# A Fourier mixer and a low-rank mixer on one core: U's rows turned by an f32 product, signed table copies on ACT, folds and column loads held in written order, three o buffers

## The chip, the cores and the metric

The kernel runs on one core of one Trainium2 chip. A core has five engines, each with its own instruction stream in order: PE (matrix products into PSUM, with the weight loads PEld beside them), DVE (elementwise work), ACT (functions and copies), POOL (elementwise work, and the issue of some transfers) and SP (the issue of transfers). Sixteen DMA engines carry the transfers of all queues. The metric is the device time in microseconds (us) of one execution; less is better.

## What is computed

For each of 8 batches of `x` (3136 rows n, 256 columns d, f32), a Fourier transform along both axes, of which the real part is kept, then a low-rank mixing over the rows, and a two-layer network over the columns:

```python
X = np.fft.fft(x, axis=1); X = np.fft.fft(X, axis=2); x = X.real
xt = x.transpose(0, 2, 1)
h = xt @ U @ V                      # U: 3136 x 32, V: 32 x 3136
u = x + h.transpose(0, 2, 1)
ch = np.maximum(u @ w_ch1, 0.0) @ w_ch2     # 256 x 1024, 1024 x 256
out = u + ch
```

## The kernel before, in words

**Setup (lines 90 to 676, an order written by hand).** The transform along the rows is a product with tables of sines (`tabs[0]`, in the profile `tabs`) and cosines (`tabs[1]`, in the profile `tabc`), eight row tiles i of 98 or 99 partitions each. DVE makes phases (`phase`, L166 and L168: `pho` for even i with 786 values, `phe` for odd i with 394), ACT their sine (L173). Other parts of the tables are copies of cells with the sign kept or changed: `mirror_even` on ACT (L255), `cosine_odd` and `cosine_turned` on POOL, where a kept sign is a copy (L260) and a changed one a multiplication by -1 (L262). For tiles 7 and 3 cosines come from ACT (L179, L180).

Symmetry halves the work: rows n and S-n are added and subtracted ("folded") before the product, and so are columns d and 256-d. So each batch of `x` is loaded twice, forward with its partitions in turned order (`xf`, by a gather with an index list that POOL issues, `load_f`), and from the other end (`xr`, plain transfers, `load_r`). The same is done for U: `UF` is gathered by POOL (two gathers, L111), `UR` is loaded by SP. `fold_u` (L191, L194) makes `GU` from both, and `transform_u` appends the transform of U to the tables in four steps: `contract` (PE, L219), `keep` (ACT, L225), `turn` (PE, L232), `evict` (ACT, L237, L238). `halve` (L243) scales tile 7 of a table.

**Per batch (`transform(b)`).** Eight fold steps: for each half a of the rows, `alone` (two columns, POOL, L284) and `along_d` (DVE, L278 and L280) on `xf` and on `xr`, then `mirror` (DVE, L287) twice; then `half` (DVE, L291) twice into `G[b % 2]`. Eight `seq` steps multiply G with the tables (PE, L328), with a copy on ACT (L332) and sums on DVE (L335 to L346). Eight `chan` steps (PE, L452 and L454; ACT, L456) and `lowrank` finish the batch. `load_x(b + 1)` stands after the folds of b.

**Chunks.** The 8 x 3136 rows of the result are 49 chunks of 512. `front(c)` makes `u` of a chunk (PE, L496; DVE, L504) and its transpose `ut` by a transfer that SP issues (L507). `first_product` (PE, L516; ACT, L518) is called eight times a chunk, `second_product` (PE, L532) four times; after every second one DVE adds `ut` to the product in `p2` and writes `o` (L538 to L541), and after the fourth SP issues the transfer of `o` to the output (L546). Of `u`, `p2` and `o` there are two buffers each, of `p1`, `ut` and the PSUM tiles called dft three.

**What sets the order.** The last loop writes chunk c's first products and chunk c-1's second products into eight slots per chunk, adds the steps that the table `due` has for each slot, and calls `front(c + 1)` at slot 3. Batch b's steps are spread evenly over slots from 8*((b-1)*3136//512)+4 to 8*(b*3136//512-1)+3, so the folds of batch 1 begin at slot 4, of batch 2 at 59 (six column steps stand ahead of them), of batch 3 at 100. Up to the end of chunk 0 the program's order is kept as written. From c == 1 on (`order.close()`) a planner may change it: for each engine it takes, when by its own estimate the engine is free, the instruction written first among those whose inputs are ready.

**Column loads.** The column 128 of batches 2 to 7 is treated apart; SP loads it with 28 transfers of single 4-byte elements (`column_loads`, L383 and L391) into `cf` and `cr`, eight in the setup and one in each slot from slot 8 on. `fl` and `flip` are 0/1 matrices with which a product turns the order of partitions (L407, L410).

Of the kernel before, what the change touches and what calls it, by code (L numbers as in the profile page):

```python
# [13 lines left out]
AL = mybir.AluOpType  # L14
# [13 lines left out]
def kernel(  # L28
# [18 lines left out]
    cpool = ctx.enter_context(tc.tile_pool(name="cpool", bufs=1))  # L47
    psum = ctx.enter_context(tc.tile_pool(name="psum", bufs=1, space=bass.MemoryType.PSUM))
# [34 lines left out]
    def load_x(b):  # L83
        for a in range(2):
# [12 lines left out]
    krow = cpool.tile([P, 2, NQ], FP32, name="krow")  # L97
# [5 lines left out]
    nc.gpsimd.iota(xidx[:], pattern=[[S // 8, B], [S // 16, 2]], base=97, channel_multiplier=-1)  # L103
    load_0f(moe_U, UF, 0, R, nc.scalar)
# [13 lines left out]
    fsel = cpool.tile([P, 2, 2, R], FP32, name="fsel")  # L118
    sel = cpool.tile([P, 2, 2 * R], BF16, name="sel")
    nc.gpsimd.iota(fsel[:], pattern=[[R, 2], [2 * R, 2], [1, R]], base=0, channel_multiplier=-1,  # L120
                   allow_small_or_imprecise_dtypes=True)
    lrow = cpool.tile([P, 2, P], FP32, name="lrow")
    pcol = cpool.tile([P, 1], FP32, name="pcol")
# [35 lines left out]
    wp = ctx.enter_context(tc.tile_pool(name="wp", bufs=2))  # L159
    setup = ExitStack()  # L160
    gen = setup.enter_context(tc.tile_pool(name="gen", bufs=2))
# [25 lines left out]
    GU = [cpool.tile([KP, 2, NI, R], BF16, name=f"gu{par}", tag=f"gu{par}") for par in range(2)]  # L187
# [62 lines left out]

    def mirror_even(t, i):

        odd_m = (i + 1) // 2 % 2 == 1
        sgn = 1.0 if odd_m == (t == 0) else -1.0
        nc.scalar.activation(cells(t, i, 0, 1, NH - 1, 1), cells(t, i, NQ - 1, -1, NH - 1, 0),  # L255
                             AF.Copy, scale=sgn)

    def pool_copy(dst, src, sgn):
        if sgn > 0:
            nc.gpsimd.tensor_copy(dst, src)  # L260
        else:
            nc.gpsimd.tensor_single_scalar(dst, src, -1.0, op=AL.mult)  # L262
# [12 lines left out]
    def along_d(a, src, dst, part):  # L275
        lo, hi = src[:, a, :, 1:128], src[:, a, :, 255:128:-1]
        if part == 0:
            nc.vector.tensor_tensor(dst[:, a, :, 1:128], lo, hi, op=AL.subtract)  # L278
        else:
            nc.vector.tensor_tensor(dst[:, a, :, 129:256], lo, hi, op=AL.add)  # L280

    def alone(a, src, dst):

        nc.gpsimd.tensor_copy(dst[:, a, :, 128:257:128], src[:, a, :, 0:129:128])  # L284

    def mirror(a, cols, op):
        nc.vector.tensor_tensor(EOS[:, a, :, cols], EOF_[:, a, :, cols],  # L287
                                EOR_[:, a, ::-1][:, :, cols], op=op)

    def half(b, par, cols):  # L290
        nc.vector.tensor_tensor(G[b % 2][par][:, :, cols], EOS[:, 0, :, cols],  # L291
                                EOS[:, 1, :, cols], op=AL.add if par == 0 else AL.subtract)
# [67 lines left out]
    fl = cpool.tile([P, 2, P], FP32, name="fl")  # L360

    def column_setup():

        nc.gpsimd.iota(fl[:, 0], pattern=[[1, P]], base=-(PQ - 1), channel_multiplier=1,
                       allow_small_or_imprecise_dtypes=True)
        nc.gpsimd.iota(fl[:, 1], pattern=[[1, P]], base=0, channel_multiplier=-1,
                       allow_small_or_imprecise_dtypes=True)

# [4 lines left out]
    def column_flips():  # L373
        nc.vector.tensor_single_scalar(flip[:], fl[:], 0.0, op=AL.is_equal)
        nc.vector.tensor_copy(flip[:KP, 0, PQ:KP], flip[:KP, 1, PQ:KP])
        nc.vector.tensor_copy(unit[:], flip[:, 1, :NB])

    def column_loads():

        for t, dst, n in ((0, cf, NI - 1), (1, cr, 0)):  # L380
            for a in range(2):
                def edge(dst=dst, n=n, a=a):
                    nc.sync.dma_start(out=dst[PQ:KP, a, n, :],  # L383
                                      in_=bass.AP(x.tensor, x.offset + (B0 * S + a * HALF) * D + P,
                                                  [[D, 1], [S * D, NB]]))
                yield edge
            for b in range(NB):
                for a in range(2):
                    def load(t=t, dst=dst, b=b, a=a):
                        n0 = 1 + a * HALF if t == 0 else S - 784 - a * HALF  # L390
                        nc.sync.dma_start(  # L391
                            out=dst[:PQ, a, :, b],
                            in_=bass.AP(x.tensor, x.offset + ((B0 + b) * S + n0) * D + P,
                                        [[8 * D, PQ], [D, NI]]))
# [339 lines left out]
```

## Time and profile before

| | us |
|---|---|
| three runs | 495.13, 502.37, 510.74 |
| median | 502.37 |
| the profiled execution | 499.26 |
| its span in the profile | 497.3 |
| PE busy in the span | 460.0 (93%) |
| DVE busy | 321.2 (65%) |
| ACT busy | 279.6 (56%) |
| POOL busy | 82.3 (17%) |
| first `pt` product (L328) starts | 28.53 |
| first first product (L516) starts | 47.87 |

The span is the time from the first to the last instruction of the profiled execution; some 2 us lie around it. Busy time of PE has matrix products that overlap, so it is not PE at its peak. In a timeline, a row gives the start and the duration in us, the engine, the line of the kernel, the operation, the tile written and the tile read, and in brackets the time that the engine had been idle and what it waited for. In a table of windows, each row gives the stretch, its length, the busy time of each engine in it, the granted clock of PE (1.00 is full speed), the share of the DMA engines that is busy, and GB/s.

### The profile page before, as it was taken

To read this page: it belongs to the slowest core of one execution; us is meant where nothing else is said; L and a number is where in the kernel's file an instruction comes from. 1 tells how busy PE (TensorE), PEld (TensorE's weight loads), DVE (VectorE), ACT (ScalarE), POOL (GpSimd) and SP (SyncE) were. 2 spreads that over 40 slices of the span, in tenths; PEclk is the share of its full clock that TensorE was granted. 3 is DMA by queue.
4 is the path that set the end of the run, shared out by engine and by line. 5 is a ranking of instruction groups with operands and counts; after the bars stand their busy time and mean duration, and the time that the engine had idled before them with its cause. 6 is when DMAs were issued, how large, how long until landed. Compare 5 with 4: busy or idle time off the path is not lost.

```text
span 497.3 us, 7932 instructions
## 1 busy us (share of the span) xinstructions
PE 460.0 (93%) x3001; PEld 288.4 (58%) x3001; DVE 321.2 (65%) x712; ACT 279.6 (56%) x531; POOL 82.3 (17%) x126
## 2 busy tenths in 40 slices
PE   0378789989999999999999999999999999999997
PEld 0133446645656666666666666666666666666665
DVE  9997978799899988793474436444534444344343
ACT  4724533745646655665557554766466555655662
POOL 8973612121222331110000000000000000000000
PEclk9999979999999999999999999999999999999999
DMA  8689797989996989425323332333322532333433
GB/s 203 155 118 220 125 183 122 223 220 220 143 307 142 253 229 275 133 66 128 81 69 107 81 110 65 84 107 86 106 65 73 119 86 65 105 86 106 129 86 127
DMA packets 103492, 67.24 MB, mean 135 GB/s; under 512 B 73572, under 2 KB 99898, under 8 KB 100302
## 3 DMA queue, kind: packets, MB, share of 16 engines
q1 hardware_dynamic: 97512, 40.50, 37.2%
q0 software_dynamic: 5920, 26.24, 20.2%
q8 instruction: 23, 0.38, 0.3%
q14 instruction: 15, 0.12, 0.1%
q10 hardware_dynamic: 22, 0.00, 0.0%
HBM read 29.33 MB, written 25.69 MB: 111 GB/s over the span
## 4 chain that ended last, share of the span: by engine, by line
PE 66%; DVE 19%; DMA 10%; issue 3%; POOL 1%; SPq 0%; DVEq 0%; ACT 0%; ACTq 0%
PE p L532 27%; PE p L516 26%; PE pt L328 7%; DMA out_dram<-o 6%; DMA xf<-in_x_dram 3%; PE ph L496 3%; DVE u L504 2%; DVE eor L278 2%; DVE eof L278 2%; DVE eor L280 2%; PE pst L452 1%; PE pst L454 1%; DVE eos L287 1%; DVE eof L280 1%; DVE phe L166 1%
## 5 line engine op out<-in xcount | busy, mean ns | idle before, releaser
L518 ACT ACTIVATE h<-p 128x512 bf16<-128x512 f32 x392 | 218.9, 597 | 141.7 <-PE p L516 141.4
L516 PE MATMUL p<-u,w 128*128 128x512 bf16 x784 | 211.3, 380 | 6.2 <-DVE u L504 6.2
L532 PE MATMUL p<-w,h 128*128 128x256 bf16 x1568 | 204.6, 273 | 0.0
L532 PEld LDWEIGHTS <-h 128*128 128x128 bf16 x1568 | 153.5, 98 | 60.6 <-issue 0.9
L516 PEld LDWEIGHTS <-w 128*128 128x128 bf16 x784 | 75.5, 98 | 70.1 <-DVE u L504 6.3
L538 DVE TENSOR_TENSOR o<-p,ut 128x4 f32<-128x4 f32 (+1 forms) x100 | 16.3, 163 | 135.1 <-PE p L532 129.7
L328 PEld LDWEIGHTS <-g 98*128 98x128 bf16 (+1 forms) x288 | 28.8, 101 | 29.2 <-DVE g L291 4.5
L541 DVE TENSOR_TENSOR o<-p,ut 128x254 f32<-128x254 f32 (+1 forms) x100 | 40.7, 407 | 0.0
L540 DVE TENSOR_TENSOR o<-p,ut 128x254 f32<-128x254 f32 (+1 forms) x100 | 40.7, 407 | 0.0
L328 PE MATMUL pt<-tabc,g 98*128 98x425 bf16 (+1 forms) x160 | 37.4, 360 | 1.9 <-DVE g L291 1.1
L504 DVE TENSOR_TENSOR u<-ph,S 128x512 bf16<-128x512 f32 (+15 forms) x64 | 35.1, 557 | 1.9 <-DMA xf<-in_x_dram 1.7
L504 DVE TENSOR_TENSOR u<-ph,T 128x512 bf16<-128x512 f32 (+15 forms) x64 | 34.9, 556 | 0.0
L332 ACT COPY ev<-pt 128x425 f32<-128x425 f32 x32 | 16.5, 515 | 31.4 <-PE pt L328 18.1
L328 PE MATMUL pt<-tabs,g 98*128 98x425 bf16 (+1 forms) x128 | 30.3, 362 | 3.0 <-DVE g L291 2.5
L496 PE MATMUL ph<-va,ta 128*128 128x512 bf16 (+18 forms) x128 | 29.6, 329 | 0.5 <-DVE B L346 0.5
L335 DVE TENSOR_TENSOR tab<-pt,ev 128x32 bf16<-128x32 f32 x32 | 6.1, 190 | 28.3 <-PE pt L328 28.2
L52 POOL DMA_INDIRECT xf<-in_x_dram,xidx x16 | 18.1, 1128 | 36.8 <-DVE eof L280 26.5
L287 DVE TENSOR_TENSOR eos<-eof,eor 99x1024 bf16<-99x1024 bf16 (+2 forms) x34 | 22.3, 688 | 0.2
L452 PE MATMUL pst<-A,mc 128*128 128x392 bf16 (+1 forms) x64 | 21.1, 330 | 1.3 <-DVE u L504 0.9
L454 PE MATMUL pst<-B,msn 128*128 128x392 bf16 (+1 forms) x64 | 21.1, 330 | 0.0
L456 ACT CAST S<-pst 128x392 bf16<-128x392 f32 (+1 forms) x32 | 15.6, 489 | 8.8 <-PE pst L454 8.6
L278 DVE TENSOR_TENSOR eof<-xf 99x1016 bf16<-99x1016 f32 x16 | 19.3, 1207 | 1.7 <-DMA xf<-in_x_dram 1.7
(126 smaller groups left out, 305.8 us busy)
## 6 DMA issues: line engine op xcount, KB each, us to landing
out_dram<-o SPq DMA_DIRECT2D x48, 512.0 KB
xr<-in_x_dram POOLq DMA_DIRECT2D x14, 784.0 KB, 8.8
xr<-in_x_dram SPq DMA_DIRECT2D x2, 784.0 KB
ut<-u SPq DMA_TRANSPOSE x49
w<-in_moe_w_ch_dram POOLq DMA_DIRECT2D x1, 512.0 KB, 6.4
out_dram<-o SPq DMA_DIRECT2D x4, 128.0 KB
va<-in_moe_V_dram POOLq DMA_DIRECT2D x2, 196.0 KB, 7.2
xf<-in_x_dram,xidx POOLq DMA_INDIRECT x16, 9.8
```

Of the source, the lines that this page charges most:

```text
L278: nc.vector.tensor_tensor(dst[:, a, :, 1:128], lo, hi, op=AL.subtract)
L287: nc.vector.tensor_tensor(EOS[:, a, :, cols], EOF_[:, a, :, cols], EOR_[:, a, ::-1][:, :, cols], op=op)
L328: nc.tensor.matmul(pt[:], g[:kp(i), i, col:col + P], tabs[t][:kp(i), i, par, :], start=(n == 0), stop=(n == len(mm) - 1))
L452: nc.tensor.matmul(pt[:, :hi - lo], MC[:, h * P:(h + 1) * P], d["A"][:, lo:hi], start=True, stop=False)
L454: nc.tensor.matmul(pt[:, :hi - lo], MSN[:, h * P:(h + 1) * P], d["B"][:, lo:hi], start=False, stop=True)
L496: nc.tensor.matmul(ph[:, col:col + hi - lo], TA[b % 2][:, s * P:(s + 1) * P], VA[b % 2][:, lo:hi], start=True, stop=True)
L504: nc.vector.tensor_tensor(u[:, s, col:col + hi - lo], ph[:, col:col + hi - lo], src, op=AL.add)
L516: nc.tensor.matmul(p1[:], W1[:, s, j * P:(j + 1) * P], k["u"][:, s, :], start=(s == 0), stop=(s == 1))
L518: LAST[0] = nc.scalar.activation(k["h"][:, j, :], p1[:], AF.Relu)
L532: nc.tensor.matmul(p2[:, t % w, :], h[:, j, rs], W2[:, j, :], start=(j == 0), stop=(j == JT - 1))
L540: nc.vector.tensor_tensor(o[:, ts, 1:P], p2[:, :w, 1:P], ut[:, ts, 1:P], op=AL.add)
L541: nc.vector.tensor_tensor(o[:, ts, P + 1:D], p2[:, :w, P + 1:D], ut[:, tT, P - 1:0:-1], op=AL.add)
```

## The change

U's forward rows come in their own order by a plain transfer of SP (no gather), and PE turns them with `fl`, a 0/1 matrix in f32, in one f32 product of 99 x 99 by 99 x 512 into PSUM (`turn_u`); `fold_u` reads that. `fl` is therefore made early (POOL writes the index values, DVE compares), and `flip` becomes a copy of it. Table copies with a changed sign run on ACT, those with a kept sign on POOL (`turned_copy`; one kept sign, of tile 3 of the cosines, on ACT), and are written in another order among the sines. Tiles that only the setup uses move from the lasting pool to the one that is closed after the setup, and `o` gets three buffers. From chunk 1 on, `pin` holds every instruction of the folds and every column load behind the instruction written just ahead of it on its engine (issue order only; it adds no wait for a result). Column loads stand in every second slot instead of every one. In `column_loads` both transfers are held.

```diff
+    wp = ctx.enter_context(tc.tile_pool(name="wp", bufs=2))
+    setup = ExitStack()
+    gen = setup.enter_context(tc.tile_pool(name="gen", bufs=2))
...
-    UF = cpool.tile([KP, 2, NI, R], FP32, name="uf")
-    UR = cpool.tile([KP, 2, NI, R], FP32, name="ur")
...
+    UF = gen.tile([KP, 2, NI, R], FP32, tag="uf", name="uf", bufs=1)
+    UR = gen.tile([KP, 2, NI, R], FP32, tag="ur", name="ur", bufs=1)
...
-    nc.sync.dma_start(out=UR[:PQ].rearrange("p a i d -> p a (i d)"),
-                      in_=bass.AP(moe_U.tensor, moe_U.offset + (S - 784) * R,
-                                  [[8 * R, PQ], [-HALF * R, 2], [1, 8 * R]]))
-    for a in range(2):
-        gather(UF[:PQ, a].rearrange("p i d -> p (i d)"), moe_U, S // 8 - 1,
-               xidx[:PQ, 0, a:a + 1], 8 * R, R)
+    for t, n0, step in ((UF, 1, HALF), (UR, S - 784, -HALF)):
+        nc.sync.dma_start(out=t[:PQ].rearrange("p a i d -> p a (i d)"),
+                          in_=bass.AP(moe_U.tensor, moe_U.offset + n0 * R,
+                                      [[8 * R, PQ], [step * R, 2], [1, 8 * R]]))
...
+    nc.gpsimd.iota(fl[:, 0], pattern=[[1, P]], base=-(PQ - 1), channel_multiplier=1,
+                   allow_small_or_imprecise_dtypes=True)
+    nc.gpsimd.iota(fl[:, 1], pattern=[[1, P]], base=0, channel_multiplier=-1,
+                   allow_small_or_imprecise_dtypes=True)
...
+    TURNED = []
+
+    def turn_u():
+        nc.vector.tensor_single_scalar(fl[:], fl[:], 0.0, op=AL.is_equal)
+        nc.vector.tensor_copy(fl[:KP, 0, PQ:KP], fl[:KP, 1, PQ:KP])
+        pf = psum.tile([KP, 2, NI, R], FP32, tag="dft", name="pf", bufs=3)
+        nc.tensor.matmul(pf.rearrange("p a i r -> p (a i r)"), fl[:KP, 0, :KP],
+                         UF.rearrange("p a i r -> p (a i r)"), start=True, stop=True)
+        TURNED.append(pf)
 
     def fold_u(typ):
         h = (uo, ue)[typ]
-        nc.vector.tensor_tensor(h[:], UF[:], UR[:, :, ::-1, :],
+        nc.vector.tensor_tensor(h[:], TURNED[0][:], UR[:, :, ::-1, :],
                                 op=AL.subtract if typ == 0 else AL.add)
...
+    def turned_copy(dst, src, sgn):
+
         if sgn > 0:
             nc.gpsimd.tensor_copy(dst, src)
         else:
-            nc.gpsimd.tensor_single_scalar(dst, src, -1.0, op=AL.mult)
+            nc.scalar.activation(dst, src, AF.Copy, scale=-1.0)
+
...
+    def mirror_even(t, i):
+
+        odd_m = (i + 1) // 2 % 2 == 1
+        turned_copy(cells(t, i, 0, 1, NH - 1, 1), cells(t, i, NQ - 1, -1, NH - 1, 0),
+                    1 if odd_m == (t == 0) else -1)
 
     def cosine_odd(i):
 
-        pool_copy(cells(1, i, 1, 1, NQ - 1, 0), cells(0, i, NQ - 2, -1, NQ - 1, 1),
-                  1 if i % 4 == 0 else -1)
-
-    def cosine_turned(i):
-
-        sgn = 1 if i == 1 else -1
-        pool_copy(cells(1, i, NH - 1, 1, NH, 1), cells(0, i, NQ - 1, -1, NH, 0), sgn)
-        pool_copy(cells(1, i, 0, 1, NH - 1, 1), cells(0, i, NH - 1, 1, NH - 1, 1), -sgn)
+        turned_copy(cells(1, i, 1, 1, NQ - 1, 0), cells(0, i, NQ - 2, -1, NQ - 1, 1),
+                    1 if i % 4 == 0 else -1)
+
+    def cosine_low(i):
+
+        turned_copy(cells(1, i, NH - 1, 1, NH, 1), cells(0, i, NQ - 1, -1, NH, 0),
+                    1 if i == 1 else -1)
+
+    def cosine_high(i):
+
+        turned_copy(cells(1, i, 0, 1, NH - 1, 1), cells(0, i, NH - 1, 1, NH - 1, 1),
+                    -1 if i == 1 else 1)
+
+    PIN = []
+
+    def pin(ins):
+
+        if PIN:
+            tc.keep_in_program_order(ins)
 
...
+            pin(nc.vector.tensor_tensor(dst[:, a, :, 1:128], lo, hi, op=AL.subtract))
...
+        pin(nc.gpsimd.tensor_copy(dst[:, a, :, 128:257:128], src[:, a, :, 0:129:128]))
...
+        pin(nc.vector.tensor_tensor(EOS[:, a, :, cols], EOF_[:, a, :, cols],
+                                    EOR_[:, a, ::-1][:, :, cols], op=op))
...
+        pin(nc.vector.tensor_tensor(G[b % 2][par][:, :, cols], EOS[:, 0, :, cols],
+                                    EOS[:, 1, :, cols], op=AL.add if par == 0 else AL.subtract))
...
-        nc.vector.tensor_single_scalar(flip[:], fl[:], 0.0, op=AL.is_equal)
-        nc.vector.tensor_copy(flip[:KP, 0, PQ:KP], flip[:KP, 1, PQ:KP])
-        nc.vector.tensor_copy(unit[:], flip[:, 1, :NB])
+        nc.vector.tensor_copy(flip[:], fl[:])
+        nc.vector.tensor_copy(unit[:], fl[:, 1, :NB])
...
+                        pin(nc.sync.dma_start(
                             out=dst[:PQ, a, :, b],
                             in_=bass.AP(x.tensor, x.offset + ((B0 + b) * S + n0) * D + P,
-                                        [[8 * D, PQ], [D, NI]]))
...
-            k["o"] = cp.tile([P, CH // P, D], FP32, tag="o", name="o", bufs=2)
+            k["o"] = cp.tile([P, CH // P, D], FP32, tag="o", name="o", bufs=3)
...
-    for m, i in enumerate(range(0, NI, 2)):
+    def odd_row(m, i):
         phase(pho[:, m], krow[:KP], ncol[:KP, i:i + 1], 15)
         sine(tabs[0][:, i, :, :NQ], pho[:, m], 15, 1)
-        cosine_odd(i)
+
+    for m, i in ((0, 0), (1, 2)):
+        odd_row(m, i)
+    cosine_odd(2)
+    for m, i in ((2, 4), (3, 6)):
+        odd_row(m, i)
+    cosine_odd(6)
     for m, i in enumerate((7, 5, 3, 1)):
         phase(phe[:, m], krow[:KP, :, NH - 1:], ncol[:KP, i:i + 1], 15)
         sine(tabs[0][:, i, :, NH - 1:NQ], phe[:, m], 15, 1)
-        mirror_even(0, i)
+        if m == 0:
+            mirror_even(0, 7)
+            turn_u()
+        if i == 5:
+            cosine_high(5)
+            mirror_even(0, 5)
+        if i == 3:
+            mirror_even(0, 3)
+    cosine_low(1)
+    mirror_even(0, 1)
+    for i in (0, 4):
+        cosine_odd(i)
     fold_u(0)
     halve(0)
...
+    us, uc = transform_u(0), transform_u(1)
+    us[0]()
+    cosine(tabs[1][:, 7, :, NH - 1:NQ], phe[:, 0], 15)
+    mirror_even(1, 7)
+    cosine(tabs[1][:, 3, :, NH - 1:NQ], phe[:, 2], 15)
+    nc.scalar.copy(cells(1, 3, 0, 1, NH - 1, 1), cells(1, 3, NQ - 1, -1, NH - 1, 0))
+    us[1]()
+    us[2]()
+    cosine_low(5)
+    cosine_high(1)
+    us[3]()
     for a in range(2):
...
-    for i in (5, 1):
-        cosine_turned(i)
     nc.gpsimd.dma_start(out=W1[:, 0, :], in_=moe_w_ch1[0:P, :])
     w1t = gen.tile([P, H], FP32, name="w1t", tag="w1t", bufs=1)
     gather(w1t[:], moe_w_ch1, D, pint[:], H, 0)
+    for a in range(2):
+        alone(a, xf, EOF_)
     nc.gpsimd.memset(VA[0][:].bitcast(I32), 0)
     nc.gpsimd.dma_start(out=VA[0][:R, :], in_=moe_V)
+    nc.gpsimd.dma_start(out=W2[:], in_=moe_w_ch2.rearrange("(j p) d -> p j d", p=P))
     column_zeros()
-    for a in range(2):
-        alone(a, xf, EOF_)
-    nc.gpsimd.dma_start(out=W2[:], in_=moe_w_ch2.rearrange("(j p) d -> p j d", p=P))
-    column_setup()
...
-    us, uc = transform_u(0), transform_u(1)
-    us[0]()
-    for m, i in ((0, 7), (2, 3)):
-        cosine(tabs[1][:, i, :, NH - 1:NQ], phe[:, m], 15)
-        mirror_even(1, i)
-        if m == 0:
-            us[1]()
-            us[2]()
-    us[3]()
...
-        due.setdefault(8 + n, []).append(step)
+        due.setdefault(8 + 2 * n, []).append(step)
     for c in range(NCH + 1):
         if c == 1:
             order.close()
             tc.no_sync_barrier()
+            PIN.append(True)
```

More of the change, by code (lines that the diff above doesn't have):

```diff
@@ L91 @@
     order.enter_context(tc.manual_schedule())
-    UF = cpool.tile([KP, 2, NI, R], FP32, name="uf")
-    UR = cpool.tile([KP, 2, NI, R], FP32, name="ur")
+    UF = gen.tile([KP, 2, NI, R], FP32, tag="uf", name="uf", bufs=1)
+    UR = gen.tile([KP, 2, NI, R], FP32, tag="ur", name="ur", bufs=1)
     xidx = cpool.tile([P, B, 2], I32, name="xidx")
-    krow = cpool.tile([P, 2, NQ], FP32, name="krow")
+    krow = gen.tile([P, 2, NQ], FP32, tag="krow", name="krow", bufs=1)
     ncol = cpool.tile([P, NI], FP32, name="ncol")
@@ L103 @@
     nc.gpsimd.iota(xidx[:], pattern=[[S // 8, B], [S // 16, 2]], base=97, channel_multiplier=-1)
+    fl = cpool.tile([P, 2, P], FP32, name="fl")
+    fsel = gen.tile([P, 2, 2, R], FP32, tag="fsel", name="fsel", bufs=1)
+    sel = gen.tile([P, 2, 2 * R], BF16, tag="sel", name="sel", bufs=1)
+    lrow = gen.tile([P, 2, P], FP32, tag="lrow", name="lrow", bufs=1)
+    pcol = gen.tile([P, 1], FP32, tag="pcol", name="pcol", bufs=1)
     load_0f(moe_U, UF, 0, R, nc.scalar)
     load_0r(moe_U, UR, 0, R, nc.scalar)
[L106 to L111 removed]
+    for t, n0, step in ((UF, 1, HALF), (UR, S - 784, -HALF)):
+        nc.sync.dma_start(out=t[:PQ].rearrange("p a i d -> p a (i d)"),
+                          in_=bass.AP(moe_U.tensor, moe_U.offset + n0 * R,
+                                      [[8 * R, PQ], [step * R, 2], [1, 8 * R]]))
     load_r(0, 0)
@@ L186 @@
     ue = gen.tile([KP, 2, NI, R], FP32, name="ue", bufs=1)
-    GU = [cpool.tile([KP, 2, NI, R], BF16, name=f"gu{par}", tag=f"gu{par}") for par in range(2)]
+    GU = [gen.tile([KP, 2, NI, R], BF16, name=f"gu{par}", tag=f"gu{par}", bufs=1) for par in range(2)]
+    TURNED = []
[6 more added lines that the diff above has]
+        TURNED.append(pf)
     def fold_u(typ):
         h = (uo, ue)[typ]
-        nc.vector.tensor_tensor(h[:], UF[:], UR[:, :, ::-1, :],
+        nc.vector.tensor_tensor(h[:], TURNED[0][:], UR[:, :, ::-1, :],
                                 op=AL.subtract if typ == 0 else AL.add)
@@ L382, in edge @@
                 def edge(dst=dst, n=n, a=a):
-                    nc.sync.dma_start(out=dst[PQ:KP, a, n, :],
-                                      in_=bass.AP(x.tensor, x.offset + (B0 * S + a * HALF) * D + P,
-                                                  [[D, 1], [S * D, NB]]))
+                    pin(nc.sync.dma_start(
+                        out=dst[PQ:KP, a, n, :],
+                        in_=bass.AP(x.tensor, x.offset + (B0 * S + a * HALF) * D + P,
+                                    [[D, 1], [S * D, NB]])))
                 yield edge
```

30 lines of the change are left out of this document (3 added, 27 removed).

## The prediction

> **What bounds the kernel now.** I read the table of windows first, because the page's 93% for PE is a mean over stages with different limits.
>
> ```profile
> core 0: us, PE busy (x) PEld busy (x) DVE busy (x) ACT busy (x) POOL busy (x), PEclk, DMA share, GB/s
> 0.00:28.50 28.50, 5.67 (x48) 2.68 (x48) 27.01 (x48) 15.32 (x25) 25.46 (x44) 1.00 0.75 168
> ...
> 47.87:64.28 16.41, 11.55 (x69) 6.55 (x67) 15.59 (x23) 9.04 (x18) 9.47 (x10) 0.94 0.87 157
> 64.28:90.00 25.72, 25.71 (x146) 14.89 (x147) 19.80 (x40) 10.44 (x20) 5.33 (x8) 0.90 0.83 159
> 90.00:110.00 20.00, 18.73 (x128) 11.92 (x125) 16.75 (x29) 12.82 (x26) 3.21 (x8) 1.00 1.01 205
> 110.00:130.00 20.00, 18.68 (x119) 10.75 (x120) 19.42 (x45) 11.60 (x22) 3.65 (x7) 1.00 1.11 190
> 130.00:150.00 20.00, 18.93 (x123) 11.50 (x121) 18.28 (x37) 9.13 (x18) 6.27 (x9) 1.00 1.03 256
> ...
> 200.00:250.00 50.00, 50.00 (x337) 32.41 (x336) 34.22 (x73) 30.27 (x58) 3.71 (x4) 1.00 0.36 95
> ```
>
> Three stages are to be seen. Up to 28.5 us DVE works 27.0 of 28.5 us and PE 5.7: the head belongs to DVE. From 47.87 to 64.28 PE is idle for 4.9 us while DVE works 15.6 of 16.4. After 64.28 PE has work all the time, except for 1.27, 1.32 and 1.07 us in the three windows of 90 to 150 and 0.2 us later. So from 64 us on there are only 3.9 us to be won, and each microsecond that DVE makes PE wait there is lost. The waits answer names what part of these 3.9 us begins with:
>
> ```profile
> DVE o L538 <- DMA out_dram<-o: 4.9, 2, 3.2
> ```
>
> Next, the timelines of DVE and POOL in the head.
>
> ```profile
> 7.67 3.82 DVE L166 TENSOR_SCALAR phe<-krow,ncol 99x394 f32<-99x394 f32 x1
> 11.53 0.87 DVE L168 TENSOR_SCALAR phe<-phe 99x394 int32<-99x394 int32 x1
> 12.32 0.99 DVE L166 TENSOR_SCALAR phe<-krow,ncol 99x394 f32<-99x394 f32 x1
> ...
> 14.96 0.42 DVE L166 TENSOR_SCALAR phe<-krow,ncol 99x394 f32<-99x394 f32 x1
> 15.41 0.37 DVE L168 TENSOR_SCALAR phe<-phe 99x394 int32<-99x394 int32 x1
> ```
>
> ```profile
> 8.25 0.83 POOL L260 COPY tabc<-tabs 99x784 bf16<-99x784 bf16 x1
> 9.07 2.20 POOL L262 TENSOR_SCALAR tabc<-tabs 99x784 bf16<-99x784 bf16 x1
> ```
>
> One line, one shape, 3.82, 0.99 and 0.42 us. The long ones lie beside POOL's copies and end with them (9.07 + 2.20 = 11.27). [...]
>
> **The head, part by part.** *Copies.* Without POOL beside them the four L166/L168 pairs on `phe` cost 0.42 + 0.37; excess now 3.40 + 0.57 + 0.60 + 0.50 = 5.1 us. After the change POOL's first copy needs the sine of row 5, so the phases run clear: -5.1. Copies still on POOL: two of 784 (0.83 to 0.95) and five of some 392 (0.63), 5.0 us, beside `gu` and `halve`, which I leave at their present times. ACT gets two negated copies of 784 between its sines, below 0.95 each (the sine row of that shape). By the rows ACT's four long sines then end near 8.8, the four short ones near 13.1, both cosines near 15.6; POOL's last table copy ends near 17.0, typ 0's contraction (1.96) runs from 14.4 to 16.4, typ 1's eviction ends near 22.3 (26.9 before).
>
> *U.* Two gathers (1.18 + 1.00) leave POOL, so x's gathers start 2.8 us earlier; one 0.45 us issue joins SP. DVE gets L374's comparison (0.29) and L375's copy (0.16): +0.45. The f32 product has no row. The bf16 one of 425 columns at the same clock costs 1.60/4 = 0.40, so 0.48 for 512; I bound it by that and by eight times it, 3.8. It can start at 8.9 and DVE wants it after three more phase pairs at 11.1, so 2.2 us are covered; I take it as hidden, the bound costs 1.6. [...] The two folds of U (0.99 each) read PSUM; nearest row, L504 from PSUM at 512: 0.68, so -0.6, between 0 and -0.8.
>
> DVE's chain to the first `pt` product: -5.1 + 0.45 - 0.6 = **-5.3**, 28.5 to about 23.2. The moved `alone`, W2 and typ 0 steps change only the order on POOL and ACT that these ends already hold; the pools' new order makes cp's first tiles wait for U's tiles, done 20 us before. That stands only if x is there: U and x of batch 0 are 3.6 MB, and the page's 203 and 155 GB/s make 3.4 MB by 18.1 us, when DVE would want xf. I allow 1 us.
>
> *What is late next.* Batch 1 of x:
>
> ```profile
> 32.81 0.58 POOL L70 DMA_DIRECT2D xr<-in_x_dram  x1 [1.90 <-DVE eor L280]
> ...
> 51.35 1.30 POOL L284 CAST eof<-xf 99x16 bf16<-99x16 f32 x1 [9.80 <-DMA xf<-in_x_dram]
> ```
>
> The first fold of batch 1 starts at 51.3, as its x lands. POOL issues these loads after 3.9 us of copies that go (15.59 to 19.54) and 0.5 us of iotas that move forward; but the list behind now starts after the last table copy, at 17.0 instead of 14.4. With 12.1 us of unchanged work they start at 29.1: -3.7, not -5.3. So I take **-4** from the head (0 to -6).
>
> **Three o buffers.** They remove DVE's 4.9 us of waiting for the output's transfer; PE's idle behind it, at most the 3.9 us above, I take as **-3.7**.
>
> **Column loads.** Ten took SP 18.45 us, 1.85 each. Four per chunk of eight slots make 7.4, with a transpose (1.25) and an output (0.53) 9.2 against a chunk of 7.37 us (L496 to L496, 472.26 to 479.63): SP falls back 1.8 us per chunk over five chunks, 9 us. A transpose's result is wanted 16 slots (14.7 us) after its `front`, 3.2 us of them landing. It fits: 0, at worst +5. Today ten in one go cost PE nothing.
>
> **Folds in written order.** Today DVE takes, whenever it is free, the first instruction in written order that is ready; the folds of later batches fill its gaps, the last at 311.9 us, long before their slots. A held fold stays behind the instruction written ahead of it: all folds of a batch become ready at their slots, and are then first in line. This trace has one such case, batch 1, whose slots come as soon as its x lands:
>
> ```profile
> 55.35 0.59 PE L496 MATMUL ph<-va,ta 128*128 128x512 bf16 x2
> ...
> 64.28 2.03 PE L516 MATMUL p<-u,w 128*128 128x512 bf16 x4 [4.86 <-DVE u L504]
> ```
>
> ```profile
> 55.88 1.30 DVE L287 TENSOR_TENSOR eos<-eof,eor 99x1024 bf16<-99x1024 bf16 x2
> ...
> 62.21 0.15 DVE L538 TENSOR_TENSOR o<-p,ut 128x4 f32<-128x4 f32 x1
> ...
> 63.55 0.68 DVE L504 TENSOR_TENSOR u<-ph,S 128x512 bf16<-128x512 f32 x1
> ```
>
> The product for `u` of chunk 2 is out at 55.9, and `u` is made at 63.55: for 7.6 us folds go ahead of it, and PE stands for 4.86 us. Behind held folds are queued the `o` evictions (p2's two buffers wait for them) and `u`; PE waits for both. The price per batch: eight L278/L280 9.07 us (51.32 to 61.61 less two mirrors), four mirrors 2.43, two evictions 1.46, `u` 1.20, in all 14.2 us from the first fold to `u` of the chunk after next (the halves, 2.28, come later). PE then has 12 slots of 7.37/8 = 0.92, 11.05 us, from `front` to that `u`, less 1.4 for the `u` ahead of the folds: 9.65. So 4.5 us are missing; the freed p2 lets PE do one pair of second products, 16 x 0.109 = 1.7 us, first. I take **2.8 us** each for batches 2 to 7, **+16.8** (bounds below).
>
> **Sum.** The profiled execution took 499.26 us (span 497.3). 499.3 - 4 - 3.7 + 16.8 = **508 us**, 1.8% over it and 1.2% over the 502.37 of the median. I count 2% as what a measurement of this kernel tells from no change, so this is "the same, on the slow side". Its own range is 500 to 515: head 0 to -6, f32 product and column loads up to +3 together, stalls 1.5 to 4 us each.
>
> **Rivals.** *The folds cost nothing* (0.20): evictions and `u` slip in ahead of them, or DVE's rest between bursts is enough. For it: DVE works only 0.5 of 200 to 450 us. Against it: 7.6 us of folds ahead of a ready `u`. 499.3 - 4 - 3.7 = **491.6**, 487 to 497.
>
> *The clock falls with each stall* (0.20), the slower side. After the 4.86 us:
>
> ```profile
> 64.30:71.00 6.70, 6.70 (x26) 3.26 (x27) 3.86 (x8) 2.22 (x4) 0.00 (x0) 0.63 0.99 209
> ```
>
> 6.7 us at 0.63 lose 2.5 us; stalls of 0.91 us left the clock at 1.00. If the limit lies below 2.8 us, six more falls add 15: **523**; with stalls of the full 4.5 us, 6 x 7.0 = 42: 534. [...]
>
> *The head gives nothing* (0.05): POOL's remaining copies stall DVE elsewhere, or x is late: **512**.
>
> **How the numbers follow.** Forecast 0.55, rivals 0.20, 0.20, 0.05. Under 489.3 (2%) lies two fifths of the first rival: 0.08. Over 509.2 lie four tenths of the forecast, the second rival and most of the third: 0.45. The rest, 0.47, is the same. The range 492 to 522 leaves out half of each of the two large rivals.
>
> **What would show it.** Right: no L166 on `phe` over 0.6 us; the first L328 near 23 us; a few L278/L280 in a row near each batch's slots until about 400 us instead of 220; before a first or second product of each of batches 2 to 7 a gap of 2 to 4 us on PE, with DVE o or u as its end; no wait of `o` for the output. Wrong: PE without gaps after 64 us, or a granted clock under 1 beside each burst. The forecast fails first if DVE's order lets `u` pass the folds.

## The result and the profile after

| | before | after |
|---|---|---|
| median of the runs side by side, us | 499.77 (495.13 to 510.74) | 520.69 (520.55 to 522.8) |
| profiled execution, us (span) | 499.26 (497.3) | 520.78 (518.8) |
| PE busy, share of the span | 93% | 90% |
| first L531 (before: L516) with `u` of chunk 2, us | 64.28 | 64.18 |

The ratio is 1.046 (95% interval 1.036 to 1.056): the changed kernel is slower. Medians here and below are of all runs, while ratios leave out runs more than 1.5% above the fastest of the same kernel. The forecast was 508 us, no change clear of noise, with 500 to 515 as its own range. The 520.8 lie outside that and inside the wider 492 to 522, which takes in half of each large rival; they are near the time of the rival in which the clock falls (523).

In the profile after, the lines are renumbered: the phases are L169/L171, the folds along D L302/L304, the mirrors L311, the halves L315, `u` L519, first and second products L531 and L547, `o` L553 to L556.

The table of windows of the kernel after (PE, PEld, DVE, ACT and POOL busy in us, then PEclk, DMA share and GB/s) shows the new loss in the stage that had none:

```profile
60.00:90.00 30.00, 25.82 (x151) 15.07 (x152) 17.36 (x41) 11.22 (x22) 3.65 (x8) 0.87 0.79 149
90.00:120.00 30.00, 30.00 (x199) 18.09 (x197) 12.34 (x37) 18.60 (x39) 0.00 (x0) 1.00 0.52 97
...
170.00:220.00 50.00, 47.23 (x312) 29.99 (x311) 32.37 (x70) 27.67 (x53) 6.52 (x10) 1.00 0.65 150
220.00:270.00 50.00, 47.23 (x303) 29.70 (x301) 34.07 (x74) 25.95 (x50) 6.53 (x10) 0.97 0.61 145
```

Before, PE was busy for all 50.00 us from 200 to 250. Now 2.77 us are missing in each such window, and in some of them the granted clock is 0.97 as well: two losses, of which one comes each time and one only sometimes. The waits name the first:

```profile
PE p L547 <- DVE o L556: 13.5, 6, 2.5
PE p L531 <- DVE u L519: 9.9, 1, 9.9
DVE eof L302 <- DMA xf<-in_x_dram: 5.1, 1, 5.1
```

Six waits for `o`, one for each of batches 2 to 7. The timelines of DVE and, behind it, of PE around the burst of batch 4:

```profile
232.67 0.68 DVE L519 TENSOR_TENSOR u<-ph,S 128x512 bf16<-128x512 f32 x1
...
233.87 1.21 DVE L302 TENSOR_TENSOR eof<-xf 99x1016 bf16<-99x1016 f32 x1
...
240.31 1.21 DVE L302 TENSOR_TENSOR eof<-xf 99x1016 bf16<-99x1016 f32 x1
241.44 1.21 DVE L304 TENSOR_TENSOR eof<-xf 99x1016 bf16<-99x1016 f32 x1
242.56 1.21 DVE L302 TENSOR_TENSOR eor<-xr 99x1016 bf16<-99x1016 f32 x1
243.69 1.21 DVE L304 TENSOR_TENSOR eor<-xr 99x1016 bf16<-99x1016 f32 x1
244.82 0.16 DVE L553 TENSOR_TENSOR o<-p,ut 128x4 f32<-128x4 f32 x1
...
246.76 0.68 DVE L519 TENSOR_TENSOR u<-ph,S 128x512 bf16<-128x512 f32 x1
```

```profile
242.20 1.04 PE L547 MATMUL p<-w,h 128*128 128x256 bf16 x8
245.69 2.53 PE L547 MATMUL p<-w,h 128*128 128x256 bf16 x11 [2.45 <-DVE o L556]
```

Four folds go without a break from 240.31 to 244.82, and the eviction of `o`, which frees a buffer of `p2`, is written behind them. PE has then done all that it has. From one `u` to the next DVE needs 14.1 us (232.67 to 246.76). That is the case foreseen from batch 1, now six times: the gaps are 1.19 + 2.81 us at batch 2, 2.45 at batches 3 to 6, 2.51 at batch 7, and 0.31 us behind each of the last five; 17.9 us in all.

The second loss, in the windows around the gap of that burst and around the one at 301.5 us:

```profile
243.24:245.41 2.17, 0.00 (x0) 0.00 (x0) 2.17 (x5) 0.00 (x0) 1.92 (x1) 1.00 0.86 244
245.41:248.82 3.41, 3.13 (x15) 2.24 (x16) 3.41 (x6) 0.00 (x0) 2.07 (x4) 0.50 0.98 311
248.82:252.24 3.42, 3.11 (x18) 1.49 (x16) 2.23 (x5) 1.95 (x4) 0.00 (x0) 1.00 1.15 235
301.52:303.97 2.45, 0.00 (x0) 0.00 (x1) 2.45 (x6) 0.00 (x0) 2.20 (x1) 1.00 0.89 260
303.97:307.40 3.43, 3.26 (x22) 2.16 (x23) 3.43 (x6) 0.50 (x2) 1.80 (x4) 1.00 0.95 313
```

Two gaps of 2.45 us: after the one the clock is at half for 3.41 us, after the other it stays whole. Four of the six bursts have such a fall (from 139.6, 245.4, 361.5 and 419.5 us). At half clock four L531 take 2.03 us (at 64.18 us), at the whole 1.03 (at 52.34). So I put each fall at half of 3.41, 1.7 us: 6.8 in all, an estimate. Behind batch 1 nothing is added. There the clock is at half for 10.24 us, where it was 6.83 before, but PE stands idle for part of that time. The window of that fall in the kernel after, and then in the kernel before:

```profile
57.68:67.92 10.24, 3.74 (x13) 1.85 (x14) 10.05 (x16) 1.19 (x2) 3.17 (x5) 0.50 1.01 248
```

```profile
62.44:69.27 6.83, 4.99 (x17) 2.38 (x18) 5.40 (x10) 1.19 (x2) 1.53 (x3) 0.50 1.02 227
```

The same estimate counts only the time in which PE works at half clock: 3.74 us after, 4.99 before. That makes 1.9 us instead of 2.5, 0.6 less.

The head went as its steps said, and yet won nothing. DVE first, then PE:

```profile
8.82 0.41 DVE L169 TENSOR_SCALAR phe<-krow,ncol 99x394 f32<-99x394 f32 x1
...
11.03 0.69 DVE L204 TENSOR_TENSOR uo<-pf,ur 99x512 f32<-99x512 f32 x1
```

```profile
9.00 2.00 PE L198 MATMUL pf<-uf,fl 99*99 99x512 f32 x2 [9.00 <-DVE fl L196]
...
24.20 1.60 PE L352 MATMUL pt<-tabs,g 98*128 98x425 bf16 x4 [2.42 <-DVE g L315]
```

The first `pt` product comes 4.3 us earlier (28.53 before), of 5.3 worked out (DVE waits 0.84 us for `xr`), and the first `ph` 5.2 us (40.12 for 45.28). Then batch 1's `x` takes it all back, in the timeline of POOL, which issues its loads and makes the first use of them (a batch's rows are read once, 3.2 MB: one half of them forward into `xf`, the other half from the other end into `xr`):

```profile
30.75 1.13 POOL L73 DMA_DIRECT2D xr<-in_x_dram  x2
...
37.93 0.66 POOL L77 DMA_DIRECT2D xf<-in_x_dram  x1
...
51.25 1.30 POOL L308 CAST eof<-xf 99x16 bf16<-99x16 f32 x1 [12.09 <-DMA xf<-in_x_dram]
```

The loads are issued 2.1 to 2.4 us earlier than before and land when they did before (51.25 for 51.35), so PE's gap before the first L531 of chunk 2 is 9.93 us instead of 4.86.

Added up: 499.3 - 0.1 (head) - 0.6 (batch 1's fall of the clock) - 3.7 (gaps of 90 to 150 gone) + 17.9 + 6.8 = 519.6 us; measured 520.8. The last 1.2 us are not traced.

### The profile page after: what moved, and what is told of

Same layout as the page of the kernel before. It is cut to its first block, busy times and chain, and to the rows that moved or that the text cites. A ratio compares the mean times of both kernels' runs of the same rounds, so it can differ in the third digit from the quotient of the medians.

```text
span 518.8 us, 7963 instructions
## 1 busy us (share of the span) xinstructions
PE 468.7 (90%) x3003; PEld 290.7 (56%) x3003; DVE 315.6 (61%) x713; ACT 279.9 (54%) x532; POOL 75.9 (15%) x123
## 4 chain that ended last, share of the span: by engine, by line
PE 70%; DVE 17%; DMA 5%; POOL 3%; issue 2%; ACT 1%; SPq 1%; DVEq 0%; ACTq 0%; POOLq 0%
PE p L547 27%; PE p L531 26%; PE pt L352 9%; DVE eof L304 3%; DVE eor L302 3%; DVE eor L304 3%; PE ph L511 3%; DVE eof L302 3%; DMA xr<-in_x_dram 3%; DMA xf<-in_x_dram 3%; PE pst L467 2%; PE pst L469 2%; DVE u L519 2%; DVE eos L311 1%; DVE o L556 1%
## 5 line engine op out<-in xcount | busy, mean ns | idle before, releaser
L531 PE MATMUL p<-u,w 128*128 128x512 bf16 x784 | 211.4, 382 | 11.5 <-DVE u L519 9.9
L547 PE MATMUL p<-w,h 128*128 128x256 bf16 x1568 | 209.5, 277 | 13.5 <-DVE o L556 13.5
L547 PEld LDWEIGHTS <-h 128*128 128x128 bf16 x1568 | 154.8, 99 | 76.3 <-DVE o L556 17.4
L531 PEld LDWEIGHTS <-w 128*128 128x128 bf16 x784 | 75.8, 98 | 75.0 <-DVE u L519 10.2
L553 DVE TENSOR_TENSOR o<-p,ut 128x4 f32<-128x4 f32 (+1 forms) x100 | 16.2, 162 | 157.1 <-PE p L547 154.2
L55 POOL DMA_INDIRECT xf<-in_x_dram,xidx x16 | 25.6, 1599 | 217.3 <-DVE eof L304 161.6
L556 DVE TENSOR_TENSOR o<-p,ut 128x254 f32<-128x254 f32 (+1 forms) x100 | 40.6, 406 | 0.0
L519 DVE TENSOR_TENSOR u<-ph,S 128x512 bf16<-128x512 f32 (+15 forms) x64 | 35.0, 556 | 1.8 <-ACT S L471 1.7
L519 DVE TENSOR_TENSOR u<-ph,T 128x512 bf16<-128x512 f32 (+15 forms) x64 | 34.9, 555 | 0.0
L302 DVE TENSOR_TENSOR eof<-xf 99x1016 bf16<-99x1016 f32 x16 | 19.3, 1208 | 5.1 <-DMA xf<-in_x_dram 5.1
L311 DVE TENSOR_TENSOR eos<-eof,eor 99x1024 bf16<-99x1024 bf16 (+2 forms) x34 | 21.2, 659 | 0.1
L302 DVE TENSOR_TENSOR eor<-xr 99x1016 bf16<-99x1016 f32 x16 | 20.0, 1249 | 0.8 <-DMA xr<-in_x_dram 0.8
```

Of the source, the lines that this page charges most:

```text
L302: pin(nc.vector.tensor_tensor(dst[:, a, :, 1:128], lo, hi, op=AL.subtract))
L519: nc.vector.tensor_tensor(u[:, s, col:col + hi - lo], ph[:, col:col + hi - lo], src, op=AL.add)
L531: nc.tensor.matmul(p1[:], W1[:, s, j * P:(j + 1) * P], k["u"][:, s, :], start=(s == 0), stop=(s == 1))
L547: nc.tensor.matmul(p2[:, t % w, :], h[:, j, rs], W2[:, j, :], start=(j == 0), stop=(j == JT - 1))
L556: nc.vector.tensor_tensor(o[:, ts, P + 1:D], p2[:, :w, P + 1:D], ut[:, tT, P - 1:0:-1], op=AL.add)
```

## The experiments

| kernel | median us | ratio to before (95%) |
|---|---|---|
| after | 520.69 | 1.046 (1.036 to 1.056) |
| e1: after, folds free | 507.31 | 1.014 (1.005 to 1.023) |
| e2: nothing held, three o, new head | 504.97 | 1.012 (1.004 to 1.020) |
| e3: nothing held, two o, new head | 502.53 | 0.997 (0.986 to 1.007) |
| e4: before, folds held | 522.3 | 1.046 (1.038 to 1.054) |
| e5: after, held folds apart | 493.53 | 0.984 (0.977 to 0.990) |
| e6: after, column loads late | 517.4 | 1.032 (1.024 to 1.039) |
| e7: e5 and e6 together | 490.13 | 0.977 (0.970 to 0.983) |
| e8: e5 with two o | 494.08 | 0.987 (0.979 to 0.994) |
| e9: e7, batch 1 apart too | 484.26 | 0.968 (0.964 to 0.971) |

The first four ran side by side on one chip, e5 to e8 on one, e9 by itself; each against the kernel before on the same chip (medians 501.43, 502.86 and 501.07). By these intervals after, e4 and e6 are more than 2% slower and e9 more than 2% faster, and e3 is within 2%; the others lie too near the 2% to call against before, and are compared here with the kernel after and with each other.

**Which part costs?** The theory was that the held folds cost everything; the rivals, that the new head or the column loads do. e1 leaves the folds free:

```
-            pin(nc.vector.tensor_tensor(dst[:, a, :, 1:128], lo, hi, op=AL.subtract))
+            nc.vector.tensor_tensor(dst[:, a, :, 1:128], lo, hi, op=AL.subtract)
...
```

and so for L304, L308, L311 and L315.

> Everything of the change but the held folds (column loads stay held and spaced, three o buffers, new head). Theory (held folds cost PE one gap per batch and most gaps cost a fall of the clock): the six gaps of batches 2 to 7 (16.3 us and six of 0.3) and the four later falls (6.8 us) go: 520.8 - 17.8 - 6.8 = 496 us, with batch 1's gap of 9.9 us still there. Rival (the column loads, spaced and held, or the third o buffer, cost the time): it stays above 512, with the gaps.

The six gaps are gone, but 507.3 is 11 us over the 496 expected. The waits view has one new gap:

```profile
ACT cb L420 <- DMA cr<-in_x_dram: 10.4, 1, 10.4
PE pc L425 <- ACT cb L420: 10.3, 1, 10.3
```

The last column loads, two slots apart and in order, go out at 117.0 us, and their copy on ACT waits for them. PE stands for 10.34 us from 114.1 us on, and behind the gap its products run at half clock (three L531 in 1.48 us at 125.11, four in 1.03 ahead of it; the granted clock is 0.91 in the mean from 90 to 150 us). With the 1.7 us that a fall was put at above, gap and clock together make 12.0 us, about what is missing. Free folds read batch 2's `x` earlier, so batch 3's loads go out from 82 us on, beside the column loads. The window of 90 to 120 us in e1:

```profile
90.00:120.00 30.00, 24.06 (x164) 15.56 (x162) 25.08 (x44) 15.79 (x32) 5.36 (x10) 0.96 1.03 196
```

The DMA share is 1.03 where after had 0.52 in the same window, and a transpose on SP's queue ahead of these loads took 8.33 us. In the kernel after the last column loads go out at 107.5, and the copy runs at 112.9 without a wait. That the loads of `x` hold up the column loads is read from these rows; no run sets it apart.

e2 frees the column loads too (every slot, in no fixed order), e3 takes the third o buffer away as well, which leaves the new head alone.

```
-            PIN.append(True)
...
-        due.setdefault(8 + 2 * n, []).append(step)
+        due.setdefault(8 + n, []).append(step)
```

> New head and three o buffers alone: nothing held, one column load per slot as before. Theory: within 2 us of the kernel with only the folds freed, 496. Rival (column loads held in every second slot cost something by themselves): 3 us or more below that kernel.

> New head alone, two o buffers. Theory (batch 1's x lands at 51 us whatever the head does, so PE's start after it does not move): 499 to 500, as before, first pt product near 24.2 and the gap before the first product of chunk 2 near 9.9 us. Rival (the head's gain arrives at the end): 494 to 495.

e2 was expected at 496 and took 505. Its waits and its DVE timeline show another price, that of free folds:

```profile
PE p L547 <- DVE o L556: 4.4, 1, 4.4
```

```profile
108.16 1.22 DVE L302 TENSOR_TENSOR eof<-xf 99x1016 bf16<-99x1016 f32 x1 [7.08 <-DMA xf<-in_x_dram]
109.29 0.16 DVE L553 TENSOR_TENSOR o<-p,ut 128x4 f32<-128x4 f32 x1
```

A fold of batch 3, placed ahead of its slot, waits 7.08 us for `x` at the head of DVE's list, and the eviction of `o` behind it comes too late by 4.41 us.

e3's time is as expected: no change. Its gap before the first L531 of chunk 2 is 9.94 us, as expected too. But its waits and its DVE timeline also show a gap that nothing foresaw:

```profile
PE pst L467 <- DVE B L370: 7.8, 1, 7.8
```

```profile
92.42 0.17 DVE L553 TENSOR_TENSOR o<-p,ut 128x4 f32<-128x4 f32 x1 [7.97 <-DMA out_dram<-o]
```

With two o buffers an eviction stands at the head of DVE's list for 7.97 us, until a transfer of the output has landed, and the work behind it reaches PE 7.76 us late. With three buffers (e1, e2, after) the waits have no row of DVE for the output.

So where a free order makes DVE stand differs between these kernels. That may be why the free ones scatter (e3 492.6 to 509.6, before 494.4 to 511.5) and the held ones don't (e4 521.1 to 524.8); that is argued, not shown.

e4 is the crossing: the kernel before with nothing but held folds.

```
+    PIN = []
+
+    def pin(ins):
+
+        if PIN:
+            tc.keep_in_program_order(ins)
...
-            nc.vector.tensor_tensor(dst[:, a, :, 1:128], lo, hi, op=AL.subtract)
+            pin(nc.vector.tensor_tensor(dst[:, a, :, 1:128], lo, hi, op=AL.subtract))
...
+            PIN.append(True)
```

> The kernel before with the folds held and nothing else. Theory: 499.3 + 17.8 + some 7 of the clock, less up to 3.7 of today's gaps: 518 to 524, gaps of 2 to 4 us at each of batches 2 to 7. Rival (folds are harmless by themselves and the gaps need the later head or the spaced column loads): below 505.

522.3 us, as expected, with the same six gaps to the hundredth. Its waits:

```profile
PE p L539 <- DVE o L548: 13.5, 6, 2.5
PE p L523 <- DVE u L511: 4.8, 1, 4.8
DVE o L545 <- DMA out_dram<-o: 3.7, 1, 3.7
```

and falls of the clock: it is 0.97 in the mean from 150 to 200 us and from 200 to 250, and 0.98 from 250 to 450, where the kernel before has 1.00. By these means some 7 us of whole clock are lost, about what four falls of 1.7 us make, an estimate. The held folds are the whole slowdown. The last line says something of the o buffers: with two of them DVE still waits 3.7 us for the output, but PE has no gap from 64 us to the first burst at 132. So these gaps go with the holding, at two buffers too.

**Is it the holding, or how close the folds stand?** e5 keeps the order fixed and writes the folds of batches 2 to 7, and the next load of `x` with them, four slots apart instead of one and a half, and earlier:

```
+        if b > 1:
+            k = 6 if b == B0 else 0
+            for n, step in enumerate(steps[k:k + 9]):
+                due.setdefault(lo - 26 + 4 * n, []).append(step)
+            steps[k:k + 9] = []
+            lo += 10
         for n, step in enumerate(steps):
             due.setdefault(lo + (hi - 1 - lo) * n // len(steps), []).append(step)
```

> The kernel after, folds still held in written order, but of batches 2 to 7 the eight folds and the load of the next batch's x are written four slots apart, from 26 slots ahead of the batch's first slot on, and its other steps begin ten slots after that slot. Theory (what costs is that eight folds come in one go, 9 to 11 us of VectorE work ahead of a ready u, not that they are held): a single pair of L302/L304 is at most 2.3 us, less than what PE has in hand, so the six gaps of 2.45 to 2.81 us, the 1.19 and the 0.31 us go (-17.8), and with them the four falls of the clock (-6.8): 520.8 - 24.6 = 496, PE without a gap over 0.6 us after batch 1's, which stays at 9 to 10 us. Rival (a held fold costs by its holding, since nothing may pass it): gaps stay before u or o, in more and smaller pieces, 510 or more.

493.5 us, against 496 and 510. The windows in which the kernel after had 47.23 us of PE are in e5:

```profile
170.00:220.00 50.00, 49.68 (x328) 32.21 (x333) 34.30 (x75) 29.89 (x57) 4.77 (x7) 1.00 0.54 141
220.00:270.00 50.00, 49.68 (x328) 32.31 (x333) 33.34 (x72) 29.89 (x57) 4.51 (x9) 1.00 0.60 136
```

PE has no gap over 0.25 us after batch 1's, and the clock is 1.00 in both windows. Holding by itself costs nothing; it cost through the DVE work that stands between one `u` and the next. (My words "in one go" for the kernel after are loose: its folds are written about one and a half slots apart, 1.35 us, and need 1.75 us each with mirrors and evictions.) e5 moves the folds earlier as well as apart; e9 below moves batch 1's apart and later. No run spaces folds and leaves them free.

**Why did the head give nothing?** e6 takes the eight early column loads out of the setup and puts all 28 into the loop:

```
     cols = list(column_loads())
-    for load in cols[:8]:
-        load()
...
-    for n, step in enumerate(cols[8:]):
-        due.setdefault(8 + 2 * n, []).append(step)
+    for n, step in enumerate(cols):
+        due.setdefault(8 + 4 * n // 3, []).append(step)
```

> The kernel after, with none of the 28 column loads ahead of the loop: all are written into its slots 8 to 44, at 4n/3. Theory (the eight early column loads, whose rows of 4-byte elements landed from 30 to 57 us here and by 33 us before, share the transfers with batch 1's x and ate the head's gain): the first L302 of batch 1 starts at 47 to 48 us instead of 51.2, the gap before L531 shrinks from 9.9 to about 6, and the time is 516 to 518. Rival (x of batch 1 is bound by its own bytes or gathers, whatever else is queued): the first L302 stays at 51, the gap at 9.9, the time at 520 to 521. Risk for either: the last column loads land after slot 52, where the columns are folded, with a gap near 125 us.

The timeline of POOL, and then that of PE, in e6:

```profile
47.78 0.26 POOL L308 CAST eof<-xf 99x16 bf16<-99x16 f32 x1 [9.19 <-DMA xf<-in_x_dram]
```

```profile
60.84 0.39 PE L531 MATMUL p<-u,w 128*128 128x512 bf16 x1 [4.77 <-DVE u L519]
```

The loads of `x` go out as in the kernel after (37.36 for 37.93), but land at 47.8 instead of 51.3. The first L531 of chunk 2 starts at 60.84 us instead of 64.18, 3.3 us earlier, and the time is 3.3 us lower: the head's gain is back. The gap itself shrinks by more, to 4.77 us from 9.93, but only because PE comes to it 1.8 us later (56.07 for 54.25). What delays PE there is not shown for e6; in e7, with the same head and column loads, the granted clock is 0.84 in the mean from 22 to 40 us, in the kernel after 1.00. (How far the loads meet differs from kernel to kernel: with the eight early ones this L531 starts between 63.0 and 65.6 us in the kernel after, e1, e2, e3, e5 and e8; without them at 60.8 in e6 and 60.9 in e7.) On SP's own queue in the kernel after one sees the other side:

```profile
27.79 17.57 SPq L406 DMA_DIRECT2D cf<-in_x_dram  x6
```

Six column loads take 17.57 us there, against 6.63 us for the six at 26.56 in the kernel before: they are in flight together with batch 1's `x`.

**Are the two causes independent, and what is a third o buffer worth?** e7 is both edits in one, e8 is e5 with `bufs=2` for `o`.

> The two edits together: folds of batches 2 to 7 held but four slots apart, and all column loads in slots 8 to 44. Theory (both causes are real and independent): 520.8 - 24.6 - 4 = 492. If only the burst is a cause: 496, as with the folds spread alone. If the late column loads cost something when the columns are folded: over 500, with a gap between 105 and 130 us.

> Folds of batches 2 to 7 held but four slots apart, and two o buffers instead of three. What the third buffer is worth where PE is otherwise without gaps: by the prediction's term 3.7 us, that is 500 with waits of o for the output and gaps of 0.3 to 1 us between 90 and 150 us. Rival (those gaps in the kernel before came of folds that ran ahead and held VectorE, and the third buffer gives nothing once folds are held): the same as with three within 1 us, 496, and no gap of PE there.

e7 takes 490.1 us, 3.4 under e5, as e6 is 3.3 under after: independent. e8 takes 494.1, e5 493.5: with held and spaced folds the third buffer gives nothing, and between 90 and 150 us PE is busy 59.5 of 60 us with two.

**Does the price model hold for batch 1?** e9 takes e7 and writes batch 1's folds two slots apart from slot 8 on, so that fewer of them stand ahead of `u` of chunk 2:

```
+        k, first, gap, rest = ((0, 8, 2, 22) if b == 1 else (6, lo - 12, 2.5, 10) if b == B0 else
+                               (0, lo - 26, 4, 10))
+        for n, step in enumerate(steps[k:k + 9]):
+            due.setdefault(first + int(gap * n), []).append(step)
+        steps[k:k + 9] = []
+        lo += rest
```

> The kernel with folds four slots apart and the column loads in slots 8 to 44, and batch 1's folds written apart too: at slots 8, 10, ... 22 instead of 4, 5, 7, ... 14, its next load at 24, the rest from slot 26; batch 2's folds 2.5 slots apart from slot 40. Theory (PE's gap is the VectorE work written between one u and the next, less what PE has in hand; it needs no burst of a special kind): of the six fold steps ahead of u of chunk 2 two are left, so the gap of 4.74 us before L531 goes to under 1 us, the clock's fall of 6.8 us at half behind it goes too (-3.4), and the time is 490.1 - 4 - 3.4 = 483. Rival (that gap is the wait for batch 1's x, which lands at 47.9 us whatever is written where): the gap stays over 3 us and the time at 489 to 491. Risk: x of batch 2 is loaded some 8 slots later, and a held fold that waits for it would hold u back, with a gap between 80 and 110 us.

The timeline of DVE in e9, between the `u` of chunk 1 and that of chunk 2:

```profile
48.96 0.68 DVE L519 TENSOR_TENSOR u<-ph,T 128x512 bf16<-128x512 f32 x1
49.56 1.20 DVE L302 TENSOR_TENSOR eof<-xf 99x1016 bf16<-99x1016 f32 x1
50.68 1.22 DVE L304 TENSOR_TENSOR eof<-xf 99x1016 bf16<-99x1016 f32 x1
51.83 1.21 DVE L302 TENSOR_TENSOR eor<-xr 99x1016 bf16<-99x1016 f32 x1
52.96 1.22 DVE L304 TENSOR_TENSOR eor<-xr 99x1016 bf16<-99x1016 f32 x1
54.10 0.15 DVE L553 TENSOR_TENSOR o<-p,ut 128x4 f32<-128x4 f32 x1
...
54.83 0.68 DVE L519 TENSOR_TENSOR u<-ph,S 128x512 bf16<-128x512 f32 x1
```

Two fold steps, an eviction, and then `u`. From 40 us on PE has no gap over 0.25 us, the clock is 0.94 in the mean from 40 to 60 us and 1.00 in every window from 60 us on, and the time is 484.3 us: 3.2% under the kernel before (ratio 0.968, 0.964 to 0.971). Of the 7.4 us expected from e7 on, 5.9 came; e7's fall of the clock was priced at 3.4 us, but behind e7's gap products ran at half clock only from 60.93 us (four L531 in 2.03 us) to about 65 (two L531 in 0.60 us at 65.51), which by the same estimate cost some 2. The time is 36 us less than that of the kernel after, with the same arithmetic.

## Why the prediction was right or wrong

Two steps of the forecast failed, and they make most of the 12 us by which it was short: the clock was taken to stay whole through stalls of 2.8 us, and it fell in four of six (6.8 us); and an earlier issue of batch 1's `x` was taken for an earlier landing (3.9 of the 4 us). The price of the held folds, the largest term, was right.

- **What bounds it.** Right: PE from 64 us on, with every microsecond of a late DVE lost. The gains and losses traced here lie in gaps of PE and in its clock.
- **DVE's chain, -5.3.** Right in its parts: `phe` at 0.41 to 0.42 us, folds of U at 0.69 (0.99 less 0.3 each). The first `pt` came 4.3 us earlier, the first `ph` 5.2. The f32 product took 2.00 us and was over at 11.00, as DVE wanted it at 11.03: hidden with nothing to spare. The trace of before had no row for it; the 2.00 us are 4.2 times the 0.48 worked out from the bf16 row, and inside the bound of eight times, a factor that no run shows.
- **What is late next, -4.** Wrong. The step that failed is "Batch 1 of x": an earlier issue was taken for as much of an earlier landing. Issue moved by 2.1 to 2.4 us, of 3.7 worked out, and landing by 0.1.
- **Column loads, 0 (at worst +5).** Wrong in the same way, and one error with the one above: SP's queue in the loop was worked out, but not that the eight early loads are now in flight beside batch 1's `x` (six take 17.57 us, 6.63 before). Without them `x` lands 3.5 us earlier and the time falls by 3.3 us (e6). That the loads ran slower in each other's company is what the rows suggest; what e6 shows is that `x` is late only with them.
- **Three o buffers, -3.7.** The gaps of 90 to 150 went, so the size was right; the cause was not. With held folds they are gone with two buffers as well (e4, e8). In the trace of before only one of them, 0.91 us at 100.2, follows a wait for the output; the others follow DVE work. With free folds it stays open what a third buffer is worth: with two, a wait for the output cost 7.76 us in e3; with three there is none, but other gaps come (e1, e2).
- **Folds in written order, +16.8.** Right: 17.9 us, 2.45 to 2.8 us per burst and 0.31 behind it, and 14.1 us from `u` to `u` where 14.2 was worked out. e4 shows it alone. What the prediction did not say is that the loss is not the holding's but the spacing's (e5).
- **The clock, kept whole in the forecast; its fall was a rival at 0.20.** Wrong, and the step that moved the time most: the forecast kept the clock whole at 2.8 us of idleness, between 0.91 us (no fall) and 4.86 (a fall) in the trace of before. What a gap between the two does that trace does not show; that 2.8 us would leave the clock whole was the author's estimate, and no run shows it. In the kernel after, four of six gaps of 2.45 to 2.81 us were followed by a fall: +6.8. Behind batch 1 its price fell by 0.6. The rival's price for six falls was 15 us; at 3.41 us of half clock each it would have been 10.

With the head at -0.1 instead of -4, the bursts at 17.9 and the clock at +6.2, the prediction's own sum gives 519.6 instead of 508 us.

## What to carry to other kernels

Work that an engine does in written order is priced between two of its urgent results: add up all that is written between one `u` and the next, and compare it with what the waiting engine has in hand; then space it, rather than only free it. Holding the order and spacing the folds gave 493.5 us, freeing them where they stood 502 to 507. When a stage ahead of a load gets faster, ask what else is in flight when the load now starts: the landing, not the issue, is what has to move (here the issue came 2.1 to 2.4 us earlier, the landing 0.1).

## What the runs showed of the hardware that was not expected

The fall of the clock behind batch 1 was long and cost little: of its 10.24 us 6.50 lay in the gap of 9.93, and the other 3.74, in which PE worked, are put at 1.9 us, half of them, an estimate from the four L531 that took 2.03 us there and 1.03 ahead of the gap.

In the kernel after the falls behind the bursts stand on a grid: they begin at 139.60, 245.41, 361.47 and 419.49 us, that is 105.81, 116.06 and 58.02 us apart, 31, 34 and 17 times 3.413, and each lasts 3.41 us. The one behind batch 1 lasts three times that, 10.24 us, and the one in the kernel before twice, 6.83. Gaps of one length differ in what follows them. The windows of the kernel after that are laid on this grid, first the four ahead of the falls, then five more around the gaps, behind which the clock stayed whole (the first of them holds the gap of 1.19 us and the start of the one of 2.81, the others two gaps of 2.45):

```profile
136.19:139.60 3.41, 1.47 (x10) 0.90 (x11) 3.41 (x6) 0.51 (x1) 3.14 (x4) 1.00 0.82 264
242.00:245.41 3.41, 1.24 (x10) 0.77 (x8) 3.41 (x6) 1.05 (x2) 1.92 (x1) 1.00 0.84 213
358.05:361.47 3.42, 0.97 (x10) 0.62 (x9) 3.42 (x7) 0.10 (x1) 2.87 (x3) 1.00 0.79 234
416.08:419.49 3.41, 0.90 (x9) 0.56 (x8) 3.41 (x7) 0.46 (x1) 0.00 (x0) 1.00 0.00 0
132.77:136.19 3.42, 1.92 (x16) 1.49 (x16) 3.42 (x6) 0.18 (x1) 2.79 (x1) 1.00 0.61 168
183.97:187.39 3.42, 2.45 (x19) 1.56 (x16) 3.42 (x4) 1.56 (x3) 0.71 (x1) 1.00 0.90 235
187.39:190.80 3.41, 1.93 (x17) 1.68 (x18) 3.41 (x8) 0.00 (x0) 3.28 (x4) 1.00 0.93 267
300.03:303.44 3.41, 1.49 (x11) 0.88 (x9) 3.41 (x5) 1.08 (x2) 1.67 (x1) 1.00 0.76 217
303.44:306.85 3.41, 2.88 (x21) 2.07 (x22) 3.41 (x7) 0.00 (x0) 2.33 (x4) 1.00 0.94 306
```

PE was idle for 1.94, 2.17, 2.45 and 2.51 us in the four windows ahead of a fall, and for 1.50, 0.97, 1.48, 1.92 and 0.53 us in the others. So of two gaps of 2.45 us the one at 301.52 cost 2.45 us, and the one at 243.24, by the 1.7 us above, 4.2. These are six gaps of one execution; where a limit lies they do not show. Nor do the runs show why the clock fell in the head of some kernels (0.84 in the mean from 22 to 40 us in e7 and 0.88 in e9, 0.91 from 30 to 50 in e1 and e2) and not in that of others (1.00 from 22 to 40 in the kernel after, 1.00 from 30 to 50 in e3 and e4).
